# The second half of a fused attention, MLP and expert kernel: another order for the expert layers' second products, their weights' maxima and splits, the gating, and the first token operands

## The chip, the cores and the metric

The kernel runs on one core of a Trainium2 chip. The metric is the device time of one execution in microseconds (us). The engines are TensorE (PE, with its weight loads listed apart as PEld), VectorE (DVE), ScalarE (ACT), GpSimd (POOL) and SyncE (SP), which issues nearly all DMAs. Each engine works through its own queue in order.

## The reference

```python
x = attention(q, k, v)                        # 4 batches, 8 heads, 576 rows, head size 64
x = moe(x)                                    # 2304 tokens, 512 -> 1536 -> 512, silu(g) * val @ w_out
logits = x @ w_gate                           # 2304 x 8: the gating of the second MoE layer
P = np.exp(logits - logits.max())
for _ in range(8):                            # Sinkhorn: rows and columns in turn
    P /= P.sum(1, keepdims=True) + 1e-09
    P /= P.sum(0, keepdims=True) + 1e-09
    P *= N / E
for e in range(E):                            # 8 experts, every token through every expert
    h = np.maximum(x @ w1[e], 0.0)            # 512 -> 1024
    out += P[:, e:e + 1] * (h @ w2[e])        # 1024 -> 512
```

## The kernel before, in words

Attention and the gated MLP (`mlp_in`, `mlp_out`, 9 blocks of 256 tokens) take the first third of the time and are not touched, but for what is put at the end of the last block. The change is in the expert layers, from about 770 us on.

An expert is worked in two halves of its hidden width, so there are 16 half-experts `h`; the tokens lie in 3 groups `g` of 768, seen as a 2x2 split of each matrix with 384 columns. A **unit** `u` is one half-expert on one group: 48 units. Both products of a unit use the Winograd form of Strassen's method: 7 products in place of 8, with sums of quarter matrices before and after. All data is f16 in two parts (high and rest), so each product is 6 matmuls per tile.

- **First layer.** A unit has two *chains* `c` (halves of the hidden width), of 7 steps each (`first_step`). A step is 6 matmuls of 128x384 from a token operand `xo` and a weight `w1` into PSUM bank X or Z; ACT and DVE then copy, add, apply ReLU and split the result into an f16 pair `h` (`operand`). The list `ahead` interleaves the end of one chain with the start of the next.
- **Second layer.** Per unit and `jj` (three strips of 128 rows) there are 7 steps (`second_step`) of 6 matmuls of 128x256, and each is evacuated by one DVE instruction of L1008, which adds coefficient times PSUM onto an f32 accumulator `acc`. Steps 0, 2, 4 and 6 of such a chain go to bank P (tag "mm", two buffers), steps 1, 3 and 5 to bank Q (tag "z2", one buffer), so a bank comes back after one other second step. There are 3 second steps for 2 first steps, `BEHIND` 7 first steps later.
- **Weights.** `weight(which, h)` is a generator in 17 pieces: load (`w1r`, `w2r`, DMA on SP), two DVE reduces over the raw weight (L739), their maximum (L744), a maximum over partitions through a matmul of L131 into the one-buffer bank "mx" and a DVE reduce of L133, the scale, four sums on POOL (L768), and seven splits, each an ACT copy (L717) and a DVE instruction (L718). `AT` says at which first step, counted from a base, each piece is written; a half-expert has 42 first steps and the next one's `w1` and `w2` are prepared in it.
- **Token operands.** `load_x(t)` transposes an operand from DRAM by three DMAs (L804) and stores it to `x2s` (L808); from the second half-expert on it is read back from there. All of this is on SP's queue. `XB` is 10 buffers.
- **Gating.** `logits(g)` after each group's first chain, then `sinkhorn()`, a generator advanced in step with `k`: eight column sums `cs`, each a matmul (L878) into bank "mx" between DVE work. `coefs` makes the factors. For the second half-expert, acc is first scaled by the first half-expert's factor (L996, DVE, 18 instructions).

PE's order is exactly the order in which the code is written (`manual_schedule`); on the other engines a scheduler sets the order, and it keeps the pieces of `weight` behind the main work of the same step (`behind`). A half-expert with its 42 first and 63 second steps is called a **period** below.

Of the kernel before, what the change touches and what calls it, by code (L numbers as in the profile page):

```python
# [12 lines left out]
ALU = mybir.AluOpType  # L13
# [6 lines left out]
def kernel(  # L20
# [752 lines left out]
            yield  # L773
        (w1, w2)[which - 1][h], (inv1, inv2)[which - 1][h] = w, inv

    AT = (0, 6, 7, 7, 9, 10, 11, 11, 12, 12, 13, 14, 15, 16, 17, 18, 19)

    w1, w2, inv1, inv2 = {}, {}, {}, {}

# [11 lines left out]
    xop = {}  # L791
    XUSE = [ORDER[j][2] for j in (0, 1, 2, 3, 4, 5, 6)]

    def load_x(t):
# [5 lines left out]
        xb = pb.tile([P, KX, TW], F16, tag="xo", name=f"xo{u}_{op}", bufs=XB)  # L800
        if u < NGR:
# [9 lines left out]
        xop[t] = xb  # L811

    for t in range(XB):
        load_x(t)
    mlp_out(NTL // 2 - 1, mlp_in(NTL // 2 - 1), pb)
    pw_cm.__exit__(None, None, None)

    pc_cm = tc.tile_pool(name="pc", bufs=1, side="right", reuse_waits="tile")
    pc = pc_cm.__enter__()
    acc = {}  # L820

    def x_of(u, op):
        return xop[u * NOP + XUSE.index(op)]

    gr = small([P, KD, E], "gr")
    nc.scalar.dma_start(out=gr, in_=moe2_w_gate.rearrange("(k p) e -> p k e", p=P))
# [6 lines left out]
    eye = identity(pc.tile([P, P], F32, tag="eye", name="eye"))  # L835

    def logits(g):

        parts = (
            [(o, kk) for o in (0, 1) for kk in range(2)],  # L840
            [(0, 0), (2, 0), (0, 1), (2, 1), (3, 0), (3, 1)],
        )
        ps = psm.tile([P, 2 * NJ, 2, E], F32, tag="mx", name=f"logits{g}", bufs=1)
        for i in range(2 * NJ):
            j, a = i // 2, i % 2
            mm = []
            for op, kk in parts[a]:
# [60 lines left out]
    def first_step(c, j):  # L908
# [28 lines left out]
        elif j == 1:  # L937
            V.tensor_tensor(st["A"], Z, st["A"], ALU.add)
            A.activation(st["A"], st["A"], AF.Relu)
            operand(u, 0, f, st["A"], V)  # L940
        elif j == 2:
            st["C"] = tmp("c")
            A.activation(st["C"], X, AF.Copy)  # L943
        elif j == 4:
            st["B"] = tmp("b")
            A.activation(st["B"], X, AF.Copy)
            V.tensor_tensor(st["B"], Z, st["B"], ALU.add)
            A.activation(st["B"], st["B"], AF.Relu)
            operand(u, 2, f, st["B"], V)
        elif j == 5:  # L950
            st["D"] = tmp("d")
            A.activation(st["D"], X, AF.Relu)
            operand(u, 1, f, st["D"], V)
        elif j == 6:
            a11, a12, a21, a22 = st["A"], st["D"], st["C"], st["B"]
            V.tensor_tensor(a21, Z, a21, ALU.add)
            A.activation(a21, a21, AF.Relu)
            s1, s2 = tmp("s1"), tmp("s2")
            G.tensor_tensor(s1, a21, a22, ALU.add)
            G.tensor_tensor(s2, s1, a11, ALU.subtract)  # L960
# [20 lines left out]
    def second_step(u, jj, j, pools):  # L981
# [4 lines left out]
        xp, zp = pools  # L986
        if j == 0:
            st["X"] = xp(f"P{u}_{jj}")[:, 0:HD]
        if j in (1, 3):
            st["Z"] = zp(f"Q{u}_{jj}_{j}")[:, 0:HD]  # L990
        ps = st["Z"] if j in (1, 3, 5) else st["X"]
        i = 2 * (g * NJ + jj) + a
        if h == 0 and j in (0, 3):
            acc[i] = pc.tile([P, DM], F32, tag=f"acc{i}", name=f"acc{i}")
        if h == 1 and j in (0, 3):
            V.tensor_scalar(acc[i], acc[i], coef[0][:, i : i + 1], None, ALU.mult)  # L996
        for n, (l, r, f) in enumerate(passes(2)):
            T.matmul(  # L998
                ps,
# [10 lines left out]
            A.activation(y, ps, AF.Copy)  # L1010
        else:
            V.tensor_tensor(y, ps, y, ALU.add)
        if h == NE - 1 and j >= 5:
# [32 lines left out]
    with tc.manual_schedule(engines={mybir.EngineType.PE}):  # L1046
        for k, (c, j) in enumerate(ahead):
# [76 lines left out]
```

## Time and profile before

| | us |
|---|---|
| runs: median (lowest to highest) | 2289.12 (2283.91 to 2292.12) |
| the profiled execution: its own time / span of the profile | 2293.65 / 2291.6 |
| PE busy, of the span | 1989.1 (87%) |
| DVE busy | 1670.3 (73%) |
| ACT busy | 1324.4 (58%) |
| POOL busy | 1310.4 (57%) |
| expert layers start on PE / end of span | 772.7 / 2291.6 |

The expert layers take two thirds of the span and repeat with the period of a half-expert: the entrance (about 770 to 930 us) holds the gating and the first half-expert, 930 to 2180 us are 13 to 14 like periods in which weights are prepared, and after 2180 us only products are left. A number in square brackets at a row of a timeline is the idle time before an instruction, and behind the arrow stands what ended it.

### The profile page before, as it was taken

To read this page: it belongs to the slowest core of one execution; us is meant where nothing else is said; L and a number is where in the kernel's file an instruction comes from. 1 tells how busy PE (TensorE), PEld (TensorE's weight loads), DVE (VectorE), ACT (ScalarE), POOL (GpSimd) and SP (SyncE) were. 2 spreads that over 40 slices of the span, in tenths; PEclk is the share of its full clock that TensorE was granted. 3 is DMA by queue.
4 is the path that set the end of the run, shared out by engine and by line. 5 is a ranking of instruction groups with operands and counts; after the bars stand their busy time and mean duration, and the time that the engine had idled before them with its cause. 6 is when DMAs were issued, how large, how long until landed. Compare 5 with 4: busy or idle time off the path is not lost.

```text
span 2291.6 us, 43968 instructions
## 1 busy us (share of the span) xinstructions
PE 1989.1 (87%) x16464; PEld 1457.2 (64%) x16464; DVE 1670.3 (73%) x3442; ACT 1324.4 (58%) x2786; POOL 1310.4 (57%) x1404
## 2 busy tenths in 40 slices
PE   1458789899999888799999998999989999999899
PEld 0236666777767555566666666666666666666677
DVE  6998777786652458777777777777777777777866
ACT  6877877877633455455555555545555555555553
POOL 1347564666643564465665666655766566566654
PEclk9869999999999989899999999999999999999999
DMA  9895888878744292333334333343333333433232
GB/s 261 198 204 100 160 150 163 169 131 143 117 110 108 63 214 84 113 111 107 109 109 127 116 102 104 107 126 112 112 121 110 107 109 109 134 108 109 84 108 79
DMA packets 372038, 286.80 MB, mean 125 GB/s; under 512 B 286064, under 2 KB 299504, under 8 KB 371824
## 3 DMA queue, kind: packets, MB, share of 16 engines
q1 hardware_dynamic: 371232, 283.97, 48.9%
q8 instruction: 129, 2.11, 0.4%
q14 instruction: 85, 0.70, 0.1%
q0 software_dynamic: 64, 0.00, 0.0%
q10 hardware_dynamic: 528, 0.02, 0.0%
HBM read 192.04 MB, written 21.23 MB: 93 GB/s over the span
## 4 chain that ended last, share of the span: by engine, by line
PE 51%; DVE 15%; POOL 3%; issue 3%; DMA 2%; ACT 1%; SPq 1%; DVEq 0%; POOLq 0%; ACTq 0%
PE P L998 14%; PE X L926 11%; PE Q L998 9%; PE Z L926 9%; DVE w L718 5%; PE gv L530 4%; DVE acc L1008 3%; DVE h L905 3%; PE x L561 2%; DVE w1m L739 1%; DVE w2m L739 1%; SPq L804 1%; DMA xo<-x2d 1%; ACT w L717 1%; DMA w1r<-in_moe_w_dram 1%
## 5 line engine op out<-in xcount | busy, mean ns | idle before, releaser
L998 PEld LDWEIGHTS <-h 128*128 128x128 f16 x6048 | 596.0, 99 | 221.3 <-issue 86.8
L926 PEld LDWEIGHTS <-w 128*128 128x128 f16 x4032 | 399.9, 99 | 211.6 <-issue 24.4
L998 PE MATMUL P<-w,h 128*128 128x256 f16 x3456 | 469.5, 275 | 55.7 <-DVE acc L1008 44.5
L926 PE MATMUL X<-xo,w 128*128 128x384 f16 x2304 | 440.1, 328 | 10.3 <-ACT u2c L943 5.9
L998 PE MATMUL Q<-w,h 128*128 128x256 f16 x2592 | 357.3, 275 | 12.2 <-DVE acc L1008 11.4
L1008 DVE SCALAR_TENSOR_TENSOR acc<-P,coef,acc 128x256 f32<-128x256 f32 x540 | 258.6, 479 | 126.6 <-PE P L998 121.5
L926 PE MATMUL Z<-xo,w 128*128 128x384 f16 x1728 | 341.5, 336 | 0.0
L304 POOL TENSOR_TENSOR hl<-e,hl 128x512 f16<-128x512 f32 x144 | 171.8, 1193 | 234.8 <-ACT hl L303 151.0
L1008 DVE SCALAR_TENSOR_TENSOR acc<-Q,coef,acc 128x256 f32<-128x256 f32 x405 | 194.1, 479 | 95.6 <-PE Q L998 89.9
L530 PE MATMUL gv<-xnT,wg 128*128 128x256 f16 x1296 | 168.2, 278 | 7.3 <-DVE u L540 6.1
L530 PE MATMUL gv<-xnT,wv 128*128 128x256 f16 x1296 | 167.5, 275 | 0.0
L330 PE MATMUL pv<-vs,eT 128*128 128x64 f16 (+1 forms) x2240 | 103.2, 201 | 53.9 <-DMA eT<-hl 47.1
L561 PE MATMUL x<-wo,tT 128*128 128x512 f16 x648 | 144.4, 379 | 1.1 <-DVE u L540 0.9
L530 PEld LDWEIGHTS <-wg 128*128 128x128 f16 x1296 | 127.0, 100 | 28.3 <-issue 8.3
L330 PEld LDWEIGHTS <-eT 128*128 128x128 f16 (+1 forms) x2240 | 91.0, 106 | 82.7 <-DMA eT<-hl 65.6
L298 DVE SCALAR_TENSOR_TENSOR e<-S,nt,e 128x576 f32<-128x576 f32 x144 | 116.4, 810 | 31.2 <-ACT e L296 30.9
L530 PEld LDWEIGHTS <-wv 128*128 128x128 f16 x1296 | 126.3, 99 | 15.8 <-issue 0.2
L292 DVE TENSOR_REDUCE nt<-S 128x1 f32<-128x576 f32 x144 | 106.9, 751 | 33.0 <-PE S L282 32.0
L296 ACT ACTIVATE e<-S,nt,c 128x576 f32<-128x576 f32 x144 | 117.8, 819 | 0.3 <-issue 0.3
L545 POOL TENSOR_TENSOR tT<-u,tT 128x256 f16<-128x256 f32 x108 | 74.1, 686 | 74.4 <-ACT tT L544 74.2
L561 PEld LDWEIGHTS <-tT 128*128 128x128 f16 x648 | 62.1, 98 | 71.9 <-issue 1.2
L303 ACT ACTIVATE hl<-e 128x576 f16<-128x576 f32 x144 | 97.0, 675 | 15.8 <-DVE e L298 9.6
(2635 smaller groups left out, 3743.8 us busy)
## 6 DMA issues: line engine op xcount, KB each, us to landing
xo<-x2s SPq DMA_DIRECT2D x315, 384.0 KB, 3.0
w1r<-in_moe_w_dram SPq DMA_DIRECT2D x16, 1024.0 KB, 5.9
w2r<-in_moe_w_dram SPq DMA_DIRECT2D x16, 1024.0 KB, 5.0
x2s<-xo SPq DMA_DIRECT2D x21, 384.0 KB, 2.8
wgatew<-in_moe_w_gate_dram SPq DMA_DIRECT2D x12, 512.0 KB, 5.9
wo<-in_moe_w_out_dram SPq DMA_DIRECT2D x12, 512.0 KB, 4.1
wvalw<-in_moe_w_val_dram SPq DMA_DIRECT2D x12, 512.0 KB, 4.7
x2d<-xs SPq DMA_DIRECT2D x24, 256.0 KB, 2.6
```

The costliest lines, as they stand in the source:

```text
L292: V.tensor_reduce(mx, sv, AX.XY, ALU.max)
L296: A.activation(ev, sv, AF.Exp, bias=nt[:, 0:1], scale=st["c2"][:, c : c + 1])
L298: V.scalar_tensor_tensor(ev, sv, nt[:, 1:2], ev, ALU.is_ge, ALU.mult, accum_out=sums[:, slot : slot + 1])
L303: A.activation(hl[:, 0:S], e, AF.Copy)
L304: G.tensor_tensor(hl[:, S + REM :], e[:, 0 : NCH * P], hl[:, 0 : NCH * P], ALU.subtract)
L330: T.matmul(o, lhsT=a, rhs=r, start=n == 0, stop=n == len(mm) - 1)
L530: T.matmul(gv[:, a, :], lhsT=w[:, l, kk, f * P : (f + 1) * P], rhs=xt[:, r * KD + kk, :], start=n == 0, stop=n == 3 * KD - 1,)
L561: T.matmul(ps, lhsT=tT[f][:, l, o : o + P], rhs=wo[:, f, r, :], start=n == 0, stop=n == 3 * KF - 1,)
L718: V.scalar_tensor_tensor(dst[1], src, s, dst[0], ALU.mult, ALU.subtract)
L926: T.matmul(ps, lhsT=w[:, a, l, kk, f * P : (f + 1) * P], rhs=xb[:, r * 2 + kk, :], start=n == 0 and j in (0, 1, 3), stop=n == 5, skip_grou ...
L998: T.matmul(ps, lhsT=hs[u, ao, f][:, l, jj * P : (jj + 1) * P], rhs=w2[h][:, bo, r, f, :], start=n == 0 and j in (0, 1, 3), stop=n == 5, sk ...
L1008: main[True] = V.scalar_tensor_tensor(y, ps, coef[h][:, i : i + 1], y, ALU.mult, ALU.add)
```

## The change

**The table `AT` and its bases.** The two reduces are two first steps apart and at steps 4 and 6 (before 6 and 7), the matmul of the maximum at 10 (before 9), the sums at 10 to 13, the splits at 14 to 23 in steps of one or two (before 13 to 19, in steps of one). The base of `w2` in a period is 21 (before 18). So a period's `w1` work lies in its steps 4 to 24 and its `w2` work in 25 to 45 (before 6 to 19 and 24 to 37).

**The second layer's order and banks.** Chains start 7 second steps apart but last 10, with steps 0, 3, 2, 5, 1, 4, 6 of a chain at places 0, 1, 3, 4, 5, 6, 9, so two chains run half a chain apart. Steps 0, 2, 4 and 6 use tag "mm" (two buffers), step 1 the one-buffer "mx" bank, steps 3 and 5 "z2". Bank "mx" so gets a second user beside the maxima and the gating.

**ReLU step 5 of a first chain.** ACT makes the f16 high part and the f32 copy straight from PSUM, and DVE makes the rest from PSUM: as many instructions as before.

**Gating and entrance.** Fourteen token operands (before ten) are issued while the MLP's last block runs, four of them into a pool of their own, `pt`; `logits(0)` and `logits(1)` stand at the end of that block; Sinkhorn advances every third first step (before two of five); the 18 scalings of acc go to ACT (`scale_acc`), one chain ahead. The output DMA is issued after steps 1 and 6 of the last chains.

```diff
-    AT = (0, 6, 7, 7, 9, 10, 11, 11, 12, 12, 13, 14, 15, 16, 17, 18, 19)
+    AT = (0, 4, 6, 8, 10, 10, 11, 13, 15, 12, 14, 16, 17, 19, 21, 23, 24)
...
-    for t in range(XB):
-        load_x(t)
-    mlp_out(NTL // 2 - 1, mlp_in(NTL // 2 - 1), pb)
+    for t in range(2 * NOP):
+        load_x(t, None if t < XB else pt)
...
+    mlp_out(NTL // 2 - 1, mlp_in(NTL // 2 - 1), pb)
+    logits(0)
+    logits(1)
...
         elif j == 5:
             st["D"] = tmp("d")
-            A.activation(st["D"], X, AF.Relu)
-            operand(u, 1, f, st["D"], V)
+            t = pc.tile([P, 2, TW], F16, tag="h", name=f"h{u}_1_{f}", bufs=26)
+            A.activation(t[:, 0], X, AF.Relu)
+            main["A"] = A.activation(st["D"], X, AF.Relu)
+            main[True] = V.scalar_tensor_tensor(t[:, 1], X, 0.0, t[:, 0], ALU.max, ALU.subtract)
...
-        ps = st["Z"] if j in (1, 3, 5) else st["X"]
+        r = {1: 1, 3: 3, 5: 3}.get(j, 0)
+        if j in (0, 1, 3):
+            st[r] = pools[min(r, 2)](f"P{u}_{jj}_{j}")[:, 0:HD]
+        ps = st[r]
-        if h == 1 and j in (0, 3):
-            V.tensor_scalar(acc[i], acc[i], coef[0][:, i : i + 1], None, ALU.mult)
...
+    p_bank, m_bank, q_bank = bank(psm, "mm", 2), bank(psm, "mx", 1), bank(psb, "z2", 1)
+    SLOT = ((0, 0), (3, 1), (2, 3), (5, 4), (1, 5), (4, 6), (6, 9))
-        later += [(u, jj, j, (x_bank, z_bank)) for jj in range(NJ) for j in range(7)]
+        for jj in range(NJ):
+            later += [(7 * (u * NJ + jj) + x, u, jj, j, ALL) for j, x in SLOT]
...
-        for which, base in ((1, 42 * (hn - 1) + 10 * (hn == 1)), (2, 42 * (hn - 1) + 18 + 6 * (hn == 1))):
+        for which, base in ((1, 42 * (hn - 1) + 14 * (hn == 1)), (2, 42 * (hn - 1) + 21 + 13 * (hn == 1))):
...
-            elif steps is not None and (k - started) * 2 % 5 < 2:
+            elif steps is not None and (k - started) % 3 == 0:
```

How the order moves, at three places. In the names, the number after a letter is the unit or chain, and the last number tells buffers apart.

DVE around the maximum of `w2` of half-expert 7, before:

```order
L739 TENSOR_REDUCE w2m_18443<-w2r7_18290 128x1
L905 TENSOR_TENSOR h19_1_1_18516<-u39d_18514,h19_1_1_18516 128x384 [waits Activation_49]
L744 TENSOR_TENSOR w2m_18443<-w2m_18443 128x1 [waits DVE_49]
L133 TENSOR_REDUCE w2mx_18523<-w2mxp_18521 128x1 [waits PE_49]
L78 TENSOR_SCALAR w2_1_i_18526<-w2mx_18523 128x1 [waits DVE_49]
```

The same place after:

```order
L739 TENSOR_REDUCE w2m_18484<-w2r7_18376 128x1
L952 TENSOR_TENSOR u40a_18501<-Z40_1_18539,u40a_18501 128x384 [waits PE_49,Pool_49]
L1021 SCALAR_TENSOR_TENSOR acc2_11627<-P18_1_3_18503,coef_18349,acc2_11627 128x256 [waits DVE_49,PE_49]
L1021 SCALAR_TENSOR_TENSOR acc2_11627<-P18_1_1_18558,coef_18349,acc2_11627 128x256 [waits PE_49]
L744 TENSOR_TENSOR w2m_18484<-w2m_18484 128x1 [waits DVE_49]
L973 TENSOR_TENSOR u39c_18432<-Z39_3_18445,u39c_18432 128x384 [waits PE_49]
L1021 SCALAR_TENSOR_TENSOR acc3_11646<-P18_1_0_18486,coef_18349,acc3_11646 128x256 [waits PE_49]
L919 TENSOR_TENSOR h20_0_0_18548<-u40a_18501,h20_0_0_18548 128x384 [waits Activation_49]
L1021 SCALAR_TENSOR_TENSOR acc4_11760<-P18_2_0_18610,coef_18349,acc4_11760 128x256 [waits PE_49]
L1021 SCALAR_TENSOR_TENSOR acc5_11769<-P18_2_3_18618,coef_18349,acc5_11769 128x256 [waits PE_49]
L133 TENSOR_REDUCE w2mx_18635<-w2mxp_18633 128x1 [waits PE_49]
```

L744 and L133 stood next to each other; now five pieces of main work stand between them.

PE at the other maximum, that of `w1` of half-expert 7, the first matmul of each step (Q and P second layer, X and Z first), before:

```order
L926 MATMUL X37_17928<-xo18_4_17491,w1_6_17023 128x384 [waits Activation_49]
...
L131 MATMUL w1mxp_18048<-ident_62,w1m_17957 128x128
...
L998 MATMUL Q17_0_3_18059<-w2_5_16408,h17_4_0_17661 128x256
...
L926 MATMUL Z37_3_18067<-xo18_2_17585,w1_6_17023 128x384
...
L998 MATMUL P17_0_17989<-w2_5_16408,h17_3_0_17667 128x256
...
L998 MATMUL Q17_0_3_18059<-w2_5_16408,h17_6_0_17670 128x256 [waits DVE_49]
```

The same place after (P for all second steps; the number behind the strip is the step that opened the bank):

```order
L940 MATMUL Z37_3_18067<-xo18_2_17587,w1_6_17083 128x384
...
L131 MATMUL w1mxp_18076<-ident_62,w1m_17925 128x128
...
L1011 MATMUL P17_0_1_18089<-w2_5_16536,h17_1_0_17605 128x256 [waits DVE_49]
...
L1011 MATMUL P17_0_0_17979<-w2_5_16536,h17_3_0_17670 128x256
...
L940 MATMUL X37_17941<-xo18_5_17637,w1_6_17083 128x384 [waits Activation_49]
```

Before, the step behind the maximum was a Q, in a bank of its own. Now it is step 1 of a chain, P17_0_1, which lies in the same bank as w1mxp and so waits for the L133 that reads it.

ACT where the splits of `w2` of half-expert 7 begin, before:

```order
L717 ACTIVATE w2_7_18614<-w2r7_18290,w2_1_s_18525 128x512 [waits DMAHW4_49]
L948 ACTIVATE u40b_18655<-u40b_18655 128x384 [waits DVE_49]
L936 ACTIVATE u41a_18686<-X41_18679 128x384 [waits PE_49]
L904 ACTIVATE h20_2_0_18659<-u40b_18655 128x384 [waits Activation_49]
L717 ACTIVATE w2_7_18614<-w2r7_18290,w2_1_s_18525 128x512 x2
L952 ACTIVATE u40d_18705<-X40_18483 128x384 [waits PE_49]
```

The same place after:

```order
L957 ACTIVATE u41c_18801<-X41_18681 128x384 [waits PE_49]
L918 ACTIVATE h20_5_0_18770<-u40s2_18762 128x384 [waits Pool_49]
L918 ACTIVATE h20_3_0_18773<-u40c_18608 128x384 [waits Pool_49]
L918 ACTIVATE h20_6_0_18776<-u40d_18707 128x384 [waits Pool_49]
L717 ACTIVATE w2_7_18742<-w2r7_18376,w2_1_s_18637 128x512 x3
L960 ACTIVATE u41b_18846<-X41_18681 128x384 [waits PE_49]
```

Splits stood there singly or in twos; three now stand in a row ahead of the copy u41b, for which the next step in bank X waits.

## Rows read from the trace of the kernel before

**Rows 1.** Windows; columns: us, busy PE, PEld, DVE, ACT, POOL, PEclk, DMA, GB/s.
```profile
930.00:2180.00 1250.00, 1142.05 (x8505) 836.09 (x8504) 947.29 (x1791) 662.05 (x1319) 780.22 (x755) 0.98 0.36 111
2180.00:2262.00 82.00, 81.77 (x627) 61.14 (x626) 50.65 (x100) 41.50 (x85) 45.40 (x50) 1.00 0.27 88
```

**Rows 2.** Waits of PE, 930 us to the end: us in total, times, longest.
```profile
PE P L998 <- DVE acc L1008: 44.5, 27, 2.5
PE w2mxp L131 <- DVE w2m L744: 32.9, 14, 2.4
PE w1mxp L131 <- DVE w1m L744: 17.7, 13, 1.4
PE Q L998 <- DVE acc L1008: 11.4, 13, 0.9
```

**Rows 3.** Timeline of PE, steps in an undisturbed stretch: start us, us, engine, line.
```profile
1513.53 1.14 PE L926 MATMUL Z<-xo,w 128*128 128x384 f16 x6
1514.50 0.82 PE L998 MATMUL Q<-w,h 128*128 128x256 f16 x6
1515.16 1.14 PE L926 MATMUL X<-xo,w 128*128 128x384 f16 x6
```

**Rows 4.** Timeline of PE, the places of one period where it waits.
```profile
1504.93 0.23 PE L131 MATMUL w2mxp<-ident,w2m 128*128 128x128 bf16 x1 [2.38 <-DVE w2m L744]
...
1505.88 2.13 PE L926 MATMUL Z<-xo,w 128*128 128x384 f16 x6
...
1527.40 0.81 PE L998 MATMUL P<-w,h 128*128 128x256 f16 x6 [2.46 <-DVE acc L1008]
...
1598.02 0.23 PE L131 MATMUL w2mxp<-ident,w2m 128*128 128x128 bf16 x1 [2.38 <-DVE w2m L744]
...
1689.44 0.23 PE L131 MATMUL w2mxp<-ident,w2m 128*128 128x128 bf16 x1 [2.38 <-DVE w2m L744]
```

**Rows 5.** Timeline of DVE around the first of these maxima.
```profile
1503.13 1.21 DVE L739 TENSOR_REDUCE w2m<-w2r 128x1 f32<-128x1024 f32 x1
...
1504.73 0.15 DVE L744 TENSOR_TENSOR w2m<-w2m 128x1 f32<-128x1 f32 x1
...
1505.20 0.29 DVE L133 TENSOR_REDUCE w2mx<-w2mxp 128x1 f32<-128x128 f32 x1 [0.32 <-PE w2mxp L131]
```

**Rows 6.** Groups by line and form, 930 to 2180 us: busy, mean ns | idle before.
```profile
L1008 DVE SCALAR_TENSOR_TENSOR acc<-P,coef,acc 128x256 f32<-128x256 f32 x484 | 231.6, 479 | 107.7 <-PE P L998 102.8
...
L718 DVE SCALAR_TENSOR_TENSOR w<-w2r,w_s,w 128x512 f16<-128x512 f32 x56 | 75.0, 1358 | 0.0
...
L718 DVE SCALAR_TENSOR_TENSOR w<-w1r,w_s,w 128x512 f16<-128x512 f32 x52 | 50.8, 977 | 7.6 <-ACT w L717 7.6
...
L718 DVE SCALAR_TENSOR_TENSOR w<-w2s,w_s,w 128x512 f16<-128x512 f32 x42 | 45.0, 1071 | 4.8 <-ACT w L717 4.5
L717 ACT ACTIVATE w<-w2r,w_s 128x512 f16<-128x512 f32 x56 | 38.5, 712 | 5.2 <-POOL w2r L768 5.2
```

**Rows 7.** Timeline, DVE and POOL, where the splits of `w2` meet its sums.
```profile
1520.25 3.43 DVE L718 SCALAR_TENSOR_TENSOR w<-w2r,w_s,w 128x512 f16<-128x512 f32 x2
...
1521.42 3.39 POOL L768 TENSOR_TENSOR w2s<-w2r,w2s 128x512 f32<-128x512 f32 x2
```

**Rows 8.** Waits of PE, 772 to 930 us (the entrance).
```profile
PE cs L878 <- DVE skc L875: 8.6, 3, 4.2
PE P L998 <- DVE acc L1012: 8.4, 2, 7.8
PE w1mxp L131 <- DVE w1m L744: 7.6, 1, 7.6
PE X L926 <- ACT u2c L943: 5.9, 1, 5.9
```

**Rows 9.** Timeline of SP's queue at the end of the MLP, and of DVE at 919 us.
```profile
712.32 2.54 SPq L804 DMA_TRANSPOSE xo<-x2d  x2
...
919.13 5.22 DVE L996 TENSOR_SCALAR acc<-acc,coef 128x512 f32<-128x512 f32 x13
```

More of the change, by code (lines that the diff above doesn't have):

```diff
@@ L792, with load_x @@
     XUSE = [ORDER[j][2] for j in (0, 1, 2, 3, 4, 5, 6)]
-    def load_x(t):
+    saved = {}
+    def load_x(t, pool=None):
         if t >= UNITS * NOP or t in xop:
@@ L799, in load_x @@
         g = u % NGR
-        xb = pb.tile([P, KX, TW], F16, tag="xo", name=f"xo{u}_{op}", bufs=XB)
-        if u < NGR:
+        if pool is None:
+            xb = pb.tile([P, KX, TW], F16, tag="xo", name=f"xo{u}_{op}", bufs=XB)
+        else:
+            xb = pool.tile([P, KX, TW], F16, tag=f"xs{t}", name=f"xs{u}_{op}")
+        if u < NGR and t not in saved:
             for jj in range(NJ):
@@ L810, in load_x @@
             nc.sync.dma_start(out=xb.rearrange("p a n -> p (a n)"), in_=x2s[g * NOP + op])
-        xop[t] = xb
-    for t in range(XB):
-        load_x(t)
-    mlp_out(NTL // 2 - 1, mlp_in(NTL // 2 - 1), pb)
[L816 to L820, printed above, removed]
+        if pool is None:
+            xop[t] = xb
+        else:
+            saved[t] = xb
+    pt_cm = tc.tile_pool(name="pt", bufs=1, side="left", reuse_waits="tile")
+    pt = pt_cm.__enter__()
+    for t in range(2 * NOP):
+        load_x(t, None if t < XB else pt)
     def x_of(u, op):
-        return xop[u * NOP + XUSE.index(op)]
+        t = u * NOP + XUSE.index(op)
+        return xop[t] if t in xop else saved[t]
     gr = small([P, KD, E], "gr")
@@ L834 @@
     V.scalar_tensor_tensor(wg2[:, :, 1], gr, gs[:, 0:1], wg2[:, :, 0], ALU.mult, ALU.subtract)
-    eye = identity(pc.tile([P, P], F32, tag="eye", name="eye"))
     def logits(g):
@@ L855, in logits @@
         V.tensor_tensor(v_, ps[:, :, 0, :], v_, ALU.add)
+    mlp_out(NTL // 2 - 1, mlp_in(NTL // 2 - 1), pb)
+    logits(0)
+    logits(1)
+    pt_cm.__exit__(None, None, None)
+    pw_cm.__exit__(None, None, None)
+    pc_cm = tc.tile_pool(name="pc", bufs=1, side="right", reuse_waits="tile")
+    pc = pc_cm.__enter__()
+    acc = {}
+    eye = identity(pc.tile([P, P], F32, tag="eye", name="eye"))
     def sinkhorn():
@@ L951, in first_step @@
             st["D"] = tmp("d")
-            A.activation(st["D"], X, AF.Relu)
-            operand(u, 1, f, st["D"], V)
+            t = pc.tile([P, 2, TW], F16, tag="h", name=f"h{u}_1_{f}", bufs=26)
+            A.activation(t[:, 0], X, AF.Relu)
+            main["A"] = A.activation(st["D"], X, AF.Relu)
+            main[True] = V.scalar_tensor_tensor(t[:, 1], X, 0.0, t[:, 0], ALU.max, ALU.subtract)
+            hs[u, 1, f] = t
         elif j == 6:
@@ L985, in second_step @@
         ao, bo, a, half = SECOND[j]
[L986 to L990, printed above, removed]
-        ps = st["Z"] if j in (1, 3, 5) else st["X"]
+        r = {1: 1, 3: 3, 5: 3}.get(j, 0)
+        if j in (0, 1, 3):
+            st[r] = pools[min(r, 2)](f"P{u}_{jj}_{j}")[:, 0:HD]
+        ps = st[r]
         i = 2 * (g * NJ + jj) + a
@@ L1012, in second_step @@
             V.tensor_tensor(y, ps, y, ALU.add)
-        if h == NE - 1 and j >= 5:
+        if h == NE - 1 and j in (1, 6):
             for rows, dst in out_rows(i):
@@ L1018, in bank, with scale_acc @@
         return lambda name: pool.tile([P, 512], F32, tag=tag, name=name, bufs=bufs)
-    x_bank, z_bank = bank(psm, "mm", 2), bank(psb, "z2", 1)
+    p_bank, m_bank, q_bank = bank(psm, "mm", 2), bank(psm, "mx", 1), bank(psb, "z2", 1)
+    x_free, z_free = bank(psb, "x1", 2), bank(psb, "z1", 2)
+    ALL = (p_bank, m_bank, q_bank)
+    SLOT = ((0, 0), (3, 1), (2, 3), (5, 4), (1, 5), (4, 6), (6, 9))
     later = []
     for u in range(UNITS - 1):
-        later += [(u, jj, j, (x_bank, z_bank)) for jj in range(NJ) for j in range(7)]
-    free = ((x_bank, z_bank), (x_bank, bank(psb, "z1", 2)), (bank(psb, "x1", 2), bank(psb, "z1", 2)))
-    later += [(UNITS - 1, jj, j, free[jj]) for j in range(7) for jj in range(NJ)]
+        for jj in range(NJ):
+            later += [(7 * (u * NJ + jj) + x, u, jj, j, ALL) for j, x in SLOT]
+    later = [n[1:] for n in sorted(later, key=lambda n: n[0])]
+    free = (ALL, (p_bank, z_free, z_free), (x_free, m_bank, z_free))
+    later += [(UNITS - 1, jj, j, free[jj]) for j, _ in SLOT for jj in range(NJ)]
+    def scale_acc(u, jj):
+        for a in range(2):
+            i = 2 * (u % NGR * NJ + jj) + a
+            A.activation(acc[i], acc[i], AF.Copy, scale=coef[0][:, i : i + 1])
     NCHAIN = 2 * UNITS
@@ L1053 @@
                 owed.append(u * NOP + j + XB)
-            if h == 0 and f == 0 and j == 6:
+            if h == 0 and f == 0 and j == 6 and g == NGR - 1:
                 logits(g)
                 gated = u
-            if h > 0 or gated >= k // 14:
+            if h != 0 or g < NGR - 1 or gated == u:
                 for t in owed:
@@ L1074 @@
             while done < min(want, len(later)):
-                n = later[done]
-                if n[1] == 0 and n[2] == 0 and n[0] % NGR == 0:
-                    hh = n[0] // NGR
+                u, jj, j, _ = n = later[done]
+                if j == 0 and jj == 0 and u % NGR == 0:
+                    hh = u // NGR
                     if hh == 1:
@@ L1082 @@
                         coef[0] = coefs(0)
+                        scale_acc(u, jj)
                     if hh > 0:
                         coef[hh] = coefs(hh)
+                if j == 0 and u // NGR == 1:
+                    m = u * NJ + jj + 1
+                    if m // NJ // NGR == 1:
+                        scale_acc(m // NJ, m % NJ)
                 second_step(*n)
```

## The prediction

> **What bounds the kernel now.** I read the windows first [rows 1]: from 930 to 2180 us PE is busy 1142.05 of 1250 us at a granted clock of 0.98, DVE 947.29, POOL 780.22, ACT 662.05. PE sets the time and 108 us of it are gaps. Once no weights are prepared (2180 to 2262 us) PE is busy 81.77 of 82 us, with the same two products; so the gaps belong to the preparation of weights. The waits of PE [rows 2] name them: 44.5 + 32.9 + 17.7 + 11.4 = 106.5 us from 930 us on, all for DVE, in four repeated forms. Per period: 2.38 us at the maximum of w2, 2.46 us for bank P among its splits [rows 4], 1.4 us at the maximum of w1, and 0.88 (Q) and about 0.78 (P) among its splits. The last is (44.5 - 14 x 2.46) / 13. In sum 7.84 us.
>
> The period confirms this. Starts of neighbouring steps lie 0.97 us apart behind a first step and 0.66 behind a second [rows 3], so 42 x 0.97 + 63 x 0.66 is about 82.3 us without a wait; with 7.84 it is 90.1, and measured are 91.42 and 93.09 us, in turn, from one w2 maximum to the next [rows 4]. The 93.09 period holds a step of 2.13 us instead of 1.14 right behind the maximum [rows 4]: a dip of the granted clock, 1.67 us dearer, in seven of fourteen.
>
> **Why DVE is late.** Without weights DVE is busy 50.65 / 82 = 0.62 us per us [rows 1]. A first step with its one and a half second steps lasts 82.3 / 42 = 1.96 us. Before, seven splits are written in seven such steps, 13.7 us: 8.5 us of DVE's main work, and for w2 4 x 1.358 + 3 x 1.071 = 8.6 us [rows 6], 17.1 together, 3.4 over (measured 2.46). For w1, at 0.977 each, 8.5 + 6.8 = 15.3, 1.6 over (measured 1.66). That fits, so I use it. At the maxima the cause is order: the second reduce (1.21 us) ends at 1504.34, L744 comes at 1504.73, and PE has been waiting for 2.38 us [rows 4, 5].
>
> **Part 1: the maxima.** The second reduce now stands at step 6 and the matmul at 10, four steps or 7.8 us; before 7 and 9, 3.9 us. The 3.9 us more is over the 2.38 and the 1.4 us waited. The order of DVE agrees: between L739 and L744 only three pieces of main work were put in. I take nothing left, 0 to 0.4. A new wait stands behind the maximum of w1: step 1 of a chain follows it in the same bank and has to wait for L133. The trace has the way there and back behind PE's matmul: 0.32 to reach DVE and 0.29 for L133 [rows 5], 0.6 us if DVE stands ready, and up to 0.48 more [rows 6] for an evacuation under way. Behind the waiting step on PE are all later products. I take 0.6.
>
> **Part 2: the splits.** They now lie in ten steps, 19.6 us, 12.1 of main work. For w2 12.1 + 8.6 = 20.7, 1.1 over; for w1 12.1 + 6.8 = 18.9, nothing over on the mean. But they still stand in clumps: in the order three L717 lie in a row on ACT (3 x 0.712 [rows 6]) ahead of a copy that PE needs to reuse X, and DVE has up to three L718 between evacuations. So I take 1.0 us for w2 (0 to 2.0) and 1.3 for w1 (0 to 2.9).
>
> The L718 of the raw w2 take 1.36 us in the mean, and a pair takes 3.43 us while POOL runs two sums of L768 in 3.39 [rows 7]. After the change the sums of w2 stand in one piece on POOL, mostly before these splits, so some L718 may get shorter, towards the 0.98 of w1. The Trainium skill, "SBUF — State Buffer", section "Who interferes with whom", says that a DVE instruction with two SBUF inputs contends with a POOL instruction that reads SBUF; the trace agrees so far as these rows go. By that rule the four splits would lose about 4 x 0.38 = 1.5 us, w2 would not be over, and the sum would be 14 us better; I leave it in the range.
>
> **Part 3: the second layer's order.** The count of second steps is the same, each still 0.66 us. A bank came back after one other second step; now after three or four, so the delay of an evacuation that PE feels starts later: about two steps, 1.3 us plus the first steps between. That works on the same waits and is in the figures above, not added. Step 5 of the first layer has as many instructions as before; its DVE part frees X later, since it reads PSUM itself: bounded by one such instruction (0.5 us) and hidden where DVE isn't behind, so nothing in the sum.
>
> **Steady sum.** After: 14 x 1.0 + 13 x (0.6 + 1.3) = 38.7 us against 106.5: **-68**. Ends: 13 x 0.6 = 8 us left, -99; and 14 x 2.0 + 13 x 3.5 = 73.5 left, -33. The clock dips follow only the 2.38 us wait, every other time, and never the 2.46; seven of 1.67 are 11.7 us. I take half: **-6** (0 to -12).
>
> **Part 4: the entrance** [rows 8]. The 7.6 us at the first w1 maximum are a load that comes late behind transposes on SP's queue; its base moves from 10 to 14, its maximum from step 19 to 24, and four operands are out of the queue before: -7.6 (0 to -7.6). Of three Sinkhorn waits, 8.6 us, spacing by 3 steps for 2.5 covers about 1 us each: -4 (0 to -8.6). The 7.8 us at the second half-expert come with 18 scalings on DVE, 13 of them in 5.22 us [rows 9]; on ACT one chain ahead only the factor and one scaling are in line: -7 (0 to -8.4). The 5.9 us for u2c end a chain over ACT and POOL whose order is unchanged: 0. Against this, logits(1) on PE now waits for the last operand that SP transposes; three transposes are 3 x 1.27 us [rows 9] and half of them may lie under logits(0): +2.5 (0 to +6). And logits(0) no longer fills gaps of the first steps, which wait for ACT: +1.5 (0 to +3). Net **-15** (-25 to -3, since not all go wrong together). For waits of new kinds (bank "mx" between step 1 and Sinkhorn in the first half-expert, the last chains) no row exists: below nothing is excluded since nothing else is taken away there; above, one wait of 0.5 to 1.0 us for each of some 14 meetings: **+5** (0 to +14).
>
> **Sum.** -68 - 6 - 15 + 5 = -84. The profiled execution took 2293.65 us and would take about 2210; the median of the runs is 4.5 us lower, so 2205.
>
> **Rivals.** *Waits only move*: ACT's three splits and DVE's clumps cost 5.5 us a period, near the upper end. For it: on ACT and DVE the total work is unchanged, and 20.7 in 19.6 us is no slack. Steady -33, dips 0, entrance -15, new +5: 2246 (2235 to 2270).
>
> *Clean*: all covered; the stretch from 2180 us shows that PE can run so. -99 - 12 - 25: about 2153.
>
> *The shared bank* (slower). Bank "mx" has one buffer and now 9 step-1 tiles and two maxima a period, so at each maximum there are two meetings, one ahead and one behind, where PE can go on only when DVE has read the bank. If DVE's queue is as late there as it was for bank P, 2.4 us [rows 4], four meetings cost 9.6 us, with 1.5 for the splits 11.1 against 7.84: 3.3 x 13.5 = +44, with entrance and new waits 2323. It decides from 1.8 us a meeting: 4 x 1.8 + 1.5 = 8.7, or 12 us above before in all, which is what the entrance and the new waits leave. Against it: DVE is less loaded there than at the old P wait, and the order shows only one close meeting a period.
>
> *The clock.* In the timeline no long step follows the waits of 2.46 and 0.9 us; behind the 2.38 one does, every other time [rows 4]. If instead each of three short waits a period brought a dip of 1.67 us, 3 x 1.67 x 13.5 = 68 us would stand where 12 stood: +56 in place of -6, 2267. The Trainium skill, "TensorE: Matmul & The Clock Gate", section "A second HAM failure mode: psum-queue depth-cycling", tells of a kernel that cycles PSUM banks and whose short idles make the clock go back and forth; by that rule three banks in turn with short waits speak for this rival. The trace so far shows it only at the longest but one wait.
>
> *The change doesn't do what it says*: the order on DVE and PE shows the pieces where they were meant to be, so this is left to the first rival.
>
> **Chances.** Forecast 0.55, waits only move 0.21, clean 0.10, clock 0.05, shared bank 0.09. The range 2150 to 2265 holds the forecast, some two thirds of each of its two neighbours and little of the rest: about 0.8. About 0.3%, 7 us, is what a measurement of this kernel can tell from no change. Only the shared bank ends near or above 2289, below its full price partly within 7 us of it, and a little of the waits that only move: faster 0.88, same 0.05, slower 0.07.
>
> **What would show it.** In the waits of PE: w2mxp and w1mxp gone; one new wait of 0.6 us on the step behind w1mxp, for L133 (more than 1.8 would be the shared bank); X waiting for an ACT copy behind L717, about 1 us, and second steps for L1021 under 1.5 us. Starts of two w2 maxima 85 to 87 us apart. No dip of the clock, or few. At the entrance, no 7.6 us at the first w1mxp, no 7.8 us at the second half-expert, a wait of 0 to 6 us at logits(1). The prediction is wrong if periods stay over 89 us, if a third bank's user turns up in the waits with more than 20 us, or if logits(1) waits over 10 us.

## The result and the profile after

The changed kernel takes 2204.3 us (2203.08 to 2204.45) against 2286.51 (2283.62 to 2292.12), a ratio of 0.9636 with an interval of 0.9615 to 0.9658. The forecast was 2205.

The page of the profile after begins so (busy us, share of the span):

```profile
PE 1966.6 (89%) x16464; PEld 1451.6 (66%) x16464; DVE 1614.1 (73%) x3424; ACT 1306.1 (59%) x2804; POOL 1324.6 (60%) x1404
```

The windows after, with the columns of [rows 1]:

```profile
930.00:2090.00 1160.00, 1117.19 (x8463) 827.69 (x8463) 900.05 (x1779) 635.04 (x1316) 793.44 (x755) 1.00 0.38 119
2090.00:2172.00 82.00, 81.45 (x625) 60.91 (x623) 51.68 (x105) 43.05 (x89) 44.80 (x48) 1.00 0.27 86
```

The steady part now has 43 us without PE in 1160, where it was 108 in 1250, and its granted clock reads 1.00 where it read 0.98. The stretch without weights is as it was.

The timeline of PE shows a whole period, from one w2 maximum to the next, and in it every row with an idle time of 0.2 us or more; it answers to [rows 4]:

```profile
1463.05 0.22 PE L131 MATMUL w2mxp<-ident,w2m 128*128 128x128 bf16 x1
...
1464.68 1.14 PE L940 MATMUL X<-xo,w 128*128 128x384 f16 x6 [0.75 <-ACT u46c L957]
...
1483.92 1.14 PE L940 MATMUL X<-xo,w 128*128 128x384 f16 x6 [1.13 <-ACT u47b L960]
...
1493.87 1.14 PE L940 MATMUL X<-xo,w 128*128 128x384 f16 x6 [0.33 <-ACT u48c L957]
...
1503.78 0.81 PE L1011 MATMUL P<-w,h 128*128 128x256 f16 x6 [0.29 <-DVE acc L1021]
...
1507.64 1.47 PE L1011 MATMUL P<-w,h 128*128 128x256 f16 x12 [0.38 <-DVE w1mx L133]
...
1536.77 1.14 PE L940 MATMUL X<-xo,w 128*128 128x384 f16 x6 [0.26 <-ACT u51c L957]
...
1549.49 0.22 PE L131 MATMUL w2mxp<-ident,w2m 128*128 128x128 bf16 x1
```

The maxima wait for nothing, no step is longer than its 1.14 us, and the period is 86.44 us. The waits are 0.75 + 1.13 + 0.33 + 0.29 + 0.38 + 0.26 = 3.14 us where they were 7.84, and four of the six are for ACT, for which no wait over 0.15 us stood in this part before.

Of the span's 90.3 us (2291.6 to 2201.3), thirteen periods between the w2 maxima of half-experts 2 and 15 give 84.9 (1206.7 to 1121.9 us). The rest is the entrance and the end. The expert layers' unbroken run of steps on PE starts 5.3 us later, at 777.95 for 772.68 (in both kernels two first steps stand ahead of it, inside the MLP). From there to the w2 maximum of half-expert 2 it is 168.4 us for 172.1, although that maximum now comes four first steps (7.9 us) later in the program. The end costs 0.9.

The start of the expert layers lies between 772.7 and 784.8 us in the profiles below, though the attention and most of the MLP are the same program in all. So beside the times of the runs the table of the experiments has, from the profiles, the time from that start to the end. Its last column is the mean over the thirteen periods between the w2 maxima of half-experts 2 and 15.

### The profile page after: what moved, and what is told of

It reads as the page before. It is cut to its first block, busy times and chain, and to the rows that moved or that the text cites. A ratio compares the mean times of both kernels' runs of the same rounds, so it can differ in the third digit from the quotient of the medians.

```text
span 2201.3 us, 43806 instructions
## 1 busy us (share of the span) xinstructions
PE 1966.6 (89%) x16464; PEld 1451.6 (66%) x16464; DVE 1614.1 (73%) x3424; ACT 1306.1 (59%) x2804; POOL 1324.6 (60%) x1404
## 4 chain that ended last, share of the span: by engine, by line
PE 38%; DVE 15%; POOL 9%; ACT 7%; issue 3%; DMA 2%; SPq 1%; POOLq 0%; DVEq 0%; ACTq 0%
PE P L1011 17%; PE X L940 9%; PE Z L940 6%; DVE w L718 5%; PE gv L530 3%; DVE acc L1021 3%; ACT h L918 2%; PE x L561 2%; DVE h L919 1%; DVE w1m L739 1%; ACT w L717 1%; POOL h L919 1%; DVE w2m L739 1%; DMA xo<-x2d 1%; DVE h L969 1%
## 5 line engine op out<-in xcount | busy, mean ns | idle before, releaser
L1011 PE MATMUL P<-w,h 128*128 128x256 f16 x6048 | 771.2, 273 | 11.0 <-DVE w1mx L133 6.3
L1021 DVE SCALAR_TENSOR_TENSOR acc<-P,coef,acc 128x256 f32<-128x256 f32 x945 | 441.5, 477 | 126.0 <-PE P L1011 116.2
L940 PE MATMUL Z<-xo,w 128*128 128x384 f16 x1728 | 328.8, 327 | 0.0
L539 DVE SCALAR_TENSOR_TENSOR u<-u,gv 128x256 f32<-128x256 f32 x108 | 44.9, 415 | 76.0 <-ACT u L538 68.9
L282 PE MATMUL S<-kT,qT 128*128 128x288 f16 (+1 forms) x320 | 65.6, 312 | 33.6 <-DVE e L298 24.5
```

The source lines that it names most:

```text
L940: T.matmul(ps, lhsT=w[:, a, l, kk, f * P : (f + 1) * P], rhs=xb[:, r * 2 + kk, :], start=n == 0 and j in (0, 1, 3), stop=n == 5, skip_grou ...
L1011: T.matmul(ps, lhsT=hs[u, ao, f][:, l, jj * P : (jj + 1) * P], rhs=w2[h][:, bo, r, f, :], start=n == 0 and j in (0, 1, 3), stop=n == 5, sk ...
L1021: main[True] = V.scalar_tensor_tensor(y, ps, coef[h][:, i : i + 1], y, ALU.mult, ALU.add)
```

## The experiments

| | us, median | ratio to before (interval) | from the expert layers' start | mean of 13 periods |
|---|---|---|---|---|
| before | 2286.5 | | 1518.9 | 92.82 |
| changed | 2204.3 | 0.9636 (0.9615 to 0.9658) | 1423.4 | 86.30 |
| e1 spacing alone | 2237.2 | 0.9765 (0.9741 to 0.9790) | 1460.5 | 88.01 |
| e2 order alone | 2273.8 | 0.9923 (0.9894 to 0.9953) | 1497.6 | 91.18 |
| e3 changed, old spacing | 2282.4 | 0.9957 (0.9937 to 0.9976) | 1499.6 | 91.95 |
| e4 changed, old order | 2221.7 | 0.9694 (0.9668 to 0.9720) | 1436.3 | 87.52 |
| e5 scalings behind | 2201.0 | 0.9598 (0.9582 to 0.9614) | 1416.1 | 86.48 |
| e6 operands late | 2209.1 | 0.9634 (0.9619 to 0.9649) | 1432.3 | 86.37 |
| e7 copy ahead of h | 2195.3 | 0.9580 (0.9566 to 0.9594) | 1412.2 | 85.84 |
| e8 other places for w2 | 2190.4 | 0.9558 (0.9544 to 0.9572) | 1406.6 | 85.14 |
| e9 gating at the old pace | 2208.8 | 0.9645 (0.9610 to 0.9680) | 1424.4 | 86.38 |
| e10 e5, e7 and e8 | 2188.7 | 0.9553 (0.9523 to 0.9583) | 1405.3 | 85.49 |
| e11 e5 and e8 | 2182.8 | 0.9526 (0.9495 to 0.9557) | 1399.1 | 85.14 |
| e12 e11, w1 too | 2188.1 | 0.9549 (0.9521 to 0.9577) | 1402.6 | 85.55 |

Each ratio is to runs of before on the same chip (medians there 2289.0, 2291.6 and 2289.5). So a difference in us between the medians of two rows can hold some us that are the chip's: e5 is 3.3 us below the changed kernel, by the ratios 8.7, and e6 is 4.8 us above it, by the ratios 0.5 below. Differences of under 5 us are read from the profiles below.

**Spacing or order?** Four kernels undo or do one of the two.

e1:
```diff
-    AT = (0, 6, 7, 7, 9, 10, 11, 11, 12, 12, 13, 14, 15, 16, 17, 18, 19)
+    AT = (0, 4, 6, 8, 10, 10, 11, 13, 15, 12, 14, 16, 17, 19, 21, 23, 24)
...
-        for which, base in ((1, 42 * (hn - 1) + 10 * (hn == 1)), (2, 42 * (hn - 1) + 18 + 6 * (hn == 1))):
+        for which, base in ((1, 42 * (hn - 1) + 14 * (hn == 1)), (2, 42 * (hn - 1) + 21 + 13 * (hn == 1))):
```


> The kernel before with nothing but the new table of places for the weights' pieces and its bases. Theory A (the spacing of maxima and splits carries the steady saving; the order of the second layer adds little): the w2 maxima come 86.5 to 88 us apart in place of 91.4 and 93.1, the waits of 2.4 and 1.4 us at the maxima are gone, no dips of the clock; 2205 to 2225 us. Rival B (the later reuse of banks in the second layer carries it, because PE then bears a late DVE): periods stay at 90 to 91 us with waits for L1008 of 2 us or more, 2260 to 2280 us.

e2 (the choice of the banks goes with it, as in the change):
```diff
...
-        later += [(u, jj, j, (x_bank, z_bank)) for jj in range(NJ) for j in range(7)]
+        for jj in range(NJ):
+            later += [(7 * (u * NJ + jj) + x, u, jj, j, ALL) for j, x in SLOT]
...
```


> The kernel before with nothing but the new order and banks of the second layer (output DMAs with it). Theory A: the waits at the maxima stay (2.4 and 1.4 us), those for banks P and Q go partly; 89 to 92 us a period, 2260 to 2285 us. Rival B: 86 to 88 us a period, 2210 to 2230 us.

e3 and e4 are the changed kernel with the first or the second of these turned round.

> The changed kernel with the old table and bases. Theory A: 89 to 92 us a period and waits of over 1.4 us at the maxima, 2255 to 2285 us. Rival B: 86.5 to 88 us, 2210 to 2225 us.

> The changed kernel with the old order and banks of the second layer. Theory A: 86.5 to 88 us a period, 2203 to 2220 us. Rival B: 89 to 91 us with waits for L1021 of 2 us or more, 2245 to 2270 us.

The spacing carries most: alone it takes 58 us out of the expert layers, the order alone 21; taken out of the changed kernel they cost 76 and 13. In the steady part the two gains add: 62.6 + 21.4 = 84.0 over thirteen periods, for 84.9 with everything. Taken out of the changed kernel they are 73.4 (e3) and 15.9 (e4). The third part that works in these periods, ReLU step 5, was not undone by itself. By the code, e4 differs in them from e1, and e3 from e2, in that step alone: 1137.8 us for 1144.1, and 1195.3 for 1185.3, where more falls of the clock hide what it does. So about 6 us of the 84.9 may be its own. Nor do spacing and order do what was expected of each. The waits of PE over these periods in e1 (columns as in [rows 2]):

```profile
PE P L998 <- DVE acc L1008: 31.9, 41, 1.2
PE Q L998 <- DVE acc L1008: 15.3, 39, 0.5
```

and in e2 (its first row holds one maximum more; in the thirteen periods it is 48.1 us):

```profile
PE w2mxp L131 <- DVE w2m L744: 50.8, 14, 3.7
PE w1mxp L131 <- DVE w1m L744: 17.7, 13, 1.4
PE P L996 <- DVE acc L1006: 10.8, 13, 0.8
```

The spacing removes the waits at the maxima whole, and with them every slow step; of the waits for P and Q, 42.0 + 11.4 us in the same thirteen periods before, 47 us stay, in many small pieces. The order does the opposite: it takes P and Q down to 10.8 us, and PE, now sooner at the w2 maximum, waits there 3.7 us in place of 2.4. Of the 42.6 us that the order takes from P and Q it gives back 17.2 at that maximum (30.9 to 48.1) and 6.0 at copies of ACT. With the maximum cleared by the spacing it gives back more, in other places: from e4 to the changed kernel the waits for P and Q fall from 43.4 to 3.8 us, those for ACT's copies of X rise from 0.6 to 30.4, and 5.0 for L133 come in. That leaves 5 us of waits; the rest of the 15.9 is PE's busy time (1090.2 to 1082.7 us) and idle times under 0.15 us, and is not explained. The timeline of e2 shows the step behind the wait at the maximum at the lower granted clock, as before the change:

```profile
1493.40 0.23 PE L131 MATMUL w2mxp<-ident,w2m 128*128 128x128 bf16 x1 [3.70 <-DVE w2m L744]
...
1494.37 2.12 PE L926 MATMUL Z<-xo,w 128*128 128x384 f16 x6
```

The periods and times of e2 and e3 are those of theory A, and e4 lies 1.7 us above its range. e1 lies 12 us above the range of theory A (2205 to 2225 us), since the waits for P and Q stayed and the entrance got no better: its first w1 maximum waits 10.2 us.

**The entrance.** Three parts were undone or put otherwise.

e5:
```diff
-        for a in range(2):
-            i = 2 * (u % NGR * NJ + jj) + a
-            A.activation(acc[i], acc[i], AF.Copy, scale=coef[0][:, i : i + 1])
+        with behind():
+            for a in range(2):
+                i = 2 * (u % NGR * NJ + jj) + a
+                A.activation(acc[i], acc[i], AF.Copy, scale=coef[0][:, i : i + 1])
```


> The changed kernel with the 18 scalings of acc on ACT tied behind the main work of their step, two at a time. Theory: the 6.96 us wait for the copy u9c at the second half-expert is ACT working through 18 scalings in one piece; spread out, it goes, with the slow steps behind it: 2193 to 2198 us. Rival: the evacuations on DVE that need a scaled acc wait in its place, PE behind them, 2201 to 2206 us.

What it undoes, in the timeline of the changed kernel, ACT and then PE:

```profile
917.99 5.61 ACT L1049 ACTIVATE acc<-acc,coef 128x512 f32<-128x512 f32 x9
...
924.53 3.15 ACT L1049 ACTIVATE acc<-acc,coef 128x512 f32<-128x512 f32 x5
...
928.26 2.55 ACT L1049 ACTIVATE acc<-acc,coef 128x512 f32<-128x512 f32 x4
...
931.12 0.47 ACT L957 ACTIVATE u9c<-X 128x384 f32<-128x384 f32 x1
...
931.65 2.08 PE L940 MATMUL X<-xo,w 128*128 128x384 f16 x6 [6.96 <-ACT u9c L957]
```

All 18 scalings are done within 13 us, in three runs with four other instructions between them, since the scheduler put them as early as their factor allowed, ahead of copies that PE waits for. Tied behind the main work they stand in twos and fours, and the wait is gone: from the start of the expert layers to the w2 maximum of half-expert 2 it is 159.6 us for 168.4. In the whole it is 7.3 us by the time from the expert layers' start; the medians show 3 us, and in its profile e5's expert layers start 5.4 us later. The theory holds for the wait; its 2193 to 2198 us were not reached, and 2201.0 is where the rival's range begins, though the rival's wait did not come.

e6 is the changed kernel with the ten early operands and the gating in the loop of before:
```diff
-    for t in range(2 * NOP):
-        load_x(t, None if t < XB else pt)
+    for t in range(XB):
+        load_x(t)
...
-    logits(0)
-    logits(1)
...
```


> The changed kernel with ten operands ahead and the gating matmuls of groups 0 and 1 back in the loop, as before. Theory: without the early operands the load of w1 stands behind their transposes again, 8 to 10 us of wait at the first w1 maximum; the MLP ends 5 us sooner; in sum 2206 to 2212 us. Rival: the later base alone covers the load, and the kernel gets better by the 5 us, 2198 to 2202 us.

Its first w1 maximum (timeline of PE; columns as before) shows that it is the operands and not the later base that cover the load:

```profile
827.00 0.29 PE L131 MATMUL w1mxp<-ident,w1m 128*128 128x128 bf16 x1 [10.32 <-DVE w1m L744]
```

In the changed kernel the same matmul has no wait at all (820.75 us): SP issues the load at 791.42 us there, in e6 at 817.83, behind transposes. The move is worth 8.9 us by the time from the expert layers' start, of which 3.3 are gating matmuls (1.66 for a group) that have only gone ahead of that start; the medians differ by 5 us, the ratios by nothing clear. That the MLP would end 5 us sooner did not come: the expert layers start at 777.04 us for 777.95.

e9:
```diff
-            elif steps is not None and (k - started) % 3 == 0:
+            elif steps is not None and (k - started) * 2 % 5 < 2:
```


> The changed kernel with Sinkhorn advanced two of five first steps, as before. Theory (part 4 of the prediction): the wider spacing takes about 1 us from each of the waits for the column sums, so without it they come to 12 to 14 us in place of 11: 2206 to 2209 us. Rival (from the trace of the changed kernel): the longest wait, 5.6 us, is DVE busy with splits of w1 that the new table puts beside Sinkhorn's last steps; at the old pace Sinkhorn is done before them, the waits come to 7 to 9 us: 2199 to 2203 us.

From the expert layers' start 1424.4 us for 1423.4: no difference. The median, 2208.8, lies in the theory's range, but its waits did not come: those for column sums are 8.6 us, as the rival had it, and the rival's time did not come either. The runs spread from 2203 to 2213, and the profiled one, the fastest of them, has a span of 2201.2 us for 2201.3; whether the 4.5 us between the medians are the change's is not shown. At the old pace the waits for column sums are fewer (11.0 to 8.6) and that for u9c shorter (7.0 to 1.6), but the factor is there sooner and ACT's scalings meet another place: the first write of an acc, for which PE waits 5.0 us. ACT and the waits of PE in e9:

```profile
910.53 6.23 ACT L1049 ACTIVATE acc<-acc,coef 128x512 f32<-128x512 f32 x10 [1.85 <-DVE coef L907]
```
```profile
PE cs L892 <- DVE skc L889: 8.6, 4, 4.8
PE P L1011 <- ACT acc L1023: 5.0, 1, 5.0
```

**The waits that are left.** The largest of a period, 1.13 us, has this ahead of it in the changed kernel (timeline of POOL and ACT):

```profile
1480.11 0.99 POOL L979 TENSOR_TENSOR u46d<-u46d,u46s 128x384 f32<-128x384 f32 x1
```
```profile
1481.13 0.52 ACT L918 ACTIVATE h<-u46d 128x384 f16<-128x384 f32 x1 [1.30 <-POOL u46d L979]
1481.56 1.93 ACT L717 ACTIVATE w<-w2r,w_s 128x512 f16<-128x512 f32 x3
1483.40 0.47 ACT L960 ACTIVATE u47b<-X 128x384 f32<-128x384 f32 x1
```

Splits written at steps 15, 16 and 17 all stand behind the last f16 copy of a chain, which waits for POOL; when it is done, three come at once, ahead of the copy u47b that frees X.

e7:
```diff
-            A.activation(st["C"], X, AF.Copy)
+            with tc.issue_after(A.activation(st["C"], X, AF.Copy).ins):
+                pay()
```
`pay` holds the four f16 pairs of the chain before whose sums POOL makes, moved here from its last step.


> The changed kernel with one order made on ACT: the copy of X at step 2 of a chain ahead of the four f16 copies of the chain before it, which wait for POOL. Theory: the 42 waits of X for L957 (17 us) are ACT standing at an f16 copy whose POOL sum is late; they go, 2187 to 2193 us. Rival: X is late for another reason on ACT or the wait goes to the next copy (L960), 2200 to 2206 us.

All waits for L957 went, 16.8 us over thirteen periods. But the waits of PE in e7 have others in their place:

```profile
PE P L1022 <- DVE acc L1032: 18.2, 25, 1.2
```

where the changed kernel had 3.8. So it gained 11 us by the profile and 9 by the runs, between the two theories: the wait has gone to the next late one, which is DVE.

e8:
```diff
+    AT2 = (0, 4, 6, 8, 10, 10, 10, 10, 10, 11, 12, 13, 14, 18, 19, 20, 21)
...
-            for x in AT:
+            for x in AT if which == 1 else AT2:
```


> The changed kernel with other places for w2's sums and splits (sums all at step 10, splits at 11, 12, 13, 14, 18, 19, 20 of 42), so that none falls right behind the last f16 copy of a chain. Theory: the 1.1 us wait for the copy L960 behind three splits goes, 2189 to 2195 us. Rival: what counts is DVE's load; four splits in four steps bring waits for L1021 of 1 us or more, 2203 to 2215 us.

As the theory had it. The same place in e8, ACT:

```profile
1474.64 0.52 ACT L919 ACTIVATE h<-u46c 128x384 f16<-128x384 f32 x1 [0.44 <-POOL u46c L979]
1475.07 0.48 ACT L961 ACTIVATE u47b<-X 128x384 f32<-128x384 f32 x1
1476.47 0.52 ACT L919 ACTIVATE h<-u46d 128x384 f16<-128x384 f32 x1 [0.92 <-POOL u46d L980]
```

No split stands there, and the copy of X comes ahead of the late f16 copy. The rival's cost showed too, but small (12.6 us for L1022 over thirteen periods, for 3.8); PE in a period of e8:

```profile
1470.19 0.81 PE L1012 MATMUL P<-w,h 128*128 128x256 f16 x6 [0.38 <-DVE acc L1022]
...
1473.23 0.81 PE L1012 MATMUL P<-w,h 128*128 128x256 f16 x6 [0.60 <-DVE acc L1022]
```

**Together.** e10 is e5, e7 and e8 in one, e11 is e5 and e8, and e12 is e11 with the new places for w1 as well.

> The changed kernel with the scalings tied behind, the copy of X ahead of the f16 copies, and the other places for w2's splits. If the three gains add (3, 9 and 14 us against 2204): 2178 us. If the gain of the copy's order only becomes waits for DVE's evacuations, as it did in part alone: 2184 to 2190 us.

> The changed kernel with the scalings tied behind and the other places for w2's splits. If both add: 85.2 us a period, 2183 to 2188 us. If the scalings only gained by chance: 2190 us.

> As the one before, with the new places for w1 as well. If w1's splits meet ACT's f16 copies as w2's did: under 85 us a period, 2178 to 2184 us. If for w1, whose splits brought waits of only 0.3 us, closer splits load DVE instead: 85.5 to 87 us, 2188 to 2205 us.

e11 is the best: 2182.8 us, the gains of e5 and e8 added. With e7's order on ACT on top (e10) the period is 85.49 for 85.14 us, with a wait of 2.0 us for an evacuation, so the second of its two forecasts holds. Closer splits of w1 (e12) bring 85.55, as the second forecast for it had it, but not for its reason: the new wait is 1.57 us a period for a copy on ACT (L957), not for an evacuation on DVE. In the window of e11 over thirteen periods, columns as in [rows 1], PE is without work 27 us of 1106, from 39 in the same part of the changed kernel:

```profile
939.00:2045.00 1106.00, 1079.11 (x8211) 802.18 (x8209) 865.54 (x1727) 620.73 (x1283) 755.89 (x726) 1.00 0.39 122
```

## Why the prediction was right, step by step

- **The number**: 2204.3 for 2205 is in part luck. The sum was -84 from the profiled execution (2293.65 us), to 2210; the profiled execution of the changed kernel took 2203.08, which is -90.6. The forecast then took 4.5 us off for the median, which came out lower before (2286.5 with one more run, for 2289.1) and above the profiled run after. By medians the change is 82.2 us.
- **What bounds it** holds: the gain lies in the waits for the weights' preparation, 84.9 of 90.3 us in the steady part.
- **Part 1, the maxima**: right. 2.38 and 1.4 us are gone, nothing is left, and it is the spacing that does it (e1 against e2). The new wait for L133 in the shared bank was taken at 0.6 and is 0.38 us, once a period.
- **Part 2, the splits**: the sum was near, the cause wrong. It held that spreading seven splits over ten steps relieves DVE, and that a count of DVE's work explains the waits for P and Q. The count was called a fit at 3.4 us over for 2.46 measured; e1 has the spreading and keeps 47 of 53.4 us. What was left after the change was forecast as 1.0 and 1.3 us; it is 1.13 us behind three splits on ACT, as the order had shown, 0.75 us for another copy near the w2 maximum that wasn't forecast, and 0.33 + 0.29 + 0.26 around w1.
- **Part 3, the order of the second layer**: this is the step that failed. Its effect was said to be in the figures of part 2 and was not added; it is what takes the waits for P and Q away (53.4 to 10.8 us alone; 43.4 in e4 to 3.8 in the changed kernel). Half or more of that comes back as waits for other things; in time it gains 16 to 21 us. The two errors cancelled, because part 2 had claimed these waits for the spacing.
- **Steady sum**: 4.7 us of waits a period went; forecast 5.0. **The dips** of the clock: taken as 11.7 us, half of it gone; they made 18 us (1206.7 less 13 x 91.42) and all went. This term was mis-sized by 12 us, because its rule was read from two periods (that the dips "follow only the 2.38 us wait, every other time, and never the 2.46"). In the thirteen periods before there are eleven dips, nine at the w2 maximum and two behind the 2.46 us wait for bank P, so four periods are of 91.42 us, seven of about 93.1 and two of 94.6 and 94.9. One of the two, timeline of PE before, with steps of up to 1.90 us that take 0.82 and 1.14 elsewhere:

```profile
1244.67 0.81 PE L998 MATMUL P<-w,h 128*128 128x256 f16 x6 [2.46 <-DVE acc L1008]
1245.33 1.47 PE L926 MATMUL X<-xo,w 128*128 128x384 f16 x6
1246.59 1.49 PE L998 MATMUL Q<-w,h 128*128 128x256 f16 x6
1247.87 1.90 PE L926 MATMUL Z<-xo,w 128*128 128x384 f16 x6
```

- **The entrance**: forecast -15, and +5 for waits of new kinds. Measured, together with the end of the program, -5.4 (90.3 less 84.9). The load of w1: right (e6). The Sinkhorn waits: wrong, -4 was forecast and 8.6 became 11.0 us, of which 2.6 are for L1025, the evacuation of a step 1 in bank "mx", so a wait of the new kind; and their pace changes nothing (e9). The scalings: wrong; 7.75 us for DVE became 6.96 us for ACT. The step "on ACT one chain ahead only the factor and one scaling are in line" was read from the code; on ACT the order is the scheduler's, and it had them all at once. logits(1): a wait of 2.0 us, forecast 2.5. The first chains without logits(0) between them: forecast +1.5, and u2c as staying; the waits for their copies on ACT came to 13.2 us (u0c 3.9, u2c 6.9) for 9.3 before, and with the gating back in the loop (e6) they are 8.7.
- **The rivals.** *Shared bank*: 0.38 us a meeting against the 1.8 from which it decides. *Clock*: no step in thirteen periods ran long, with six waits of 0.26 to 1.13 us in each; the reason given against it, no long step behind 2.46 us, was misread (see the dips). So the rule of the Trainium skill ("TensorE: Matmul & The Clock Gate", section "A second HAM failure mode: psum-queue depth-cycling") did not show here: three banks in turn with short idles kept the granted clock at 1.00. *Waits only move*: true in part for e2 and e7, at the scalings and in e9, but not for the whole.
- **The L718 beside POOL's sums** (the Trainium skill, "SBUF — State Buffer", section "Who interferes with whom"): with the sums mostly ahead of them, the splits of w2 take 1132 and 799 ns in the mean, for 1358 and 1071 [rows 6]. That agrees, about 1.7 us of DVE a period. The splits of the raw w1 went the other way, from 977 to 1130 ns, and those of its sums from 940 to 855, so 1.4 us a period are left in sum. Taken one by one in the traces, from 930 to 2080 us, every split with no POOL instruction beside it takes 733 to 744 ns (50 of 173 before, 52 of 183 after), and the others 1250 ns in the mean before and 1101 after. That it turned into time is not shown: what was left at that place was ACT's.

## What to carry to other kernels

A wait on the engine that sets the time goes to the next late thing as soon as the first is cured: the order took some 40 us of waits away, with the old spacing as with the new, and half or more of it came back as other waits. So undo each part by itself, and read its worth from the period and not from the wait that is gone. In code whose order a scheduler decides, read from the order, and not from the code, where work lands that was put on another engine: eighteen scalings that were meant to trickle came within 13 us. Small work put beside a main chain should keep away from the instruction on its engine that waits for a third engine, since everything behind that one bunches up (e8 moved the sums and splits of w2 and gained 14 us). A rule read from two periods has to be counted over all of them before it goes into a sum: there were eleven dips of the clock where seven had been taken.

## What the runs showed of the hardware

**The granted clock.** It has two levels in these traces, full and half (2.4 and 1.2 GHz), and between the w2 maxima of half-experts 2 and 15 every fall to the lower one stands at a wait of PE of 1.96 us or more. Before, there are eleven: nine of the fourteen waits of 1.96 to 2.38 us at the w2 maximum have one, and two of the thirteen of 2.46 us for bank P. In e2 it is ten of fourteen (2.7 to 3.7 us), in e3 all thirteen of 3.7 us. e10 has a single one, behind one of its twelve waits of 2.0 us for an evacuation:

```profile
1047.16 1.44 PE L1023 MATMUL P<-w,h 128*128 128x256 f16 x6 [2.00 <-DVE acc L1033]
1048.39 2.12 PE L952 MATMUL X<-xo,w 128*128 128x384 f16 x6
```

No shorter wait has one, up to the twelve of 1.58 us in e12 and the thirteen of 1.36 us at the w1 maximum before; and in the changed kernel and all others but e2, e3 and e10 no step of this part ran long. So the falls go with the length of the wait and not with one place. Why one such wait has a fall and the next has none is not shown. The falls cost 18 us before and 19 in e2 (1185.3 less 13 x 89.74).

**DVE beside POOL.** A split of 128x512 (L718, with two inputs in SBUF) takes 736 ns in the median with no POOL instruction beside it, before and after the change; with one it takes 1250 ns in the mean before and 1101 after.
